# A hardware-queue fp32 front, a reordered first batch and later transposes in a beacon-attention and GEGLU kernel

## The chip, the cores and the metric

The kernel runs on one core of a Trainium2 chip. The metric is the device time of one execution in microseconds. The kernel before takes 397.61 us (median of 3 runs, 397.56 to 398.33). A run is called slow when it is over 1.5% above the fastest of the same kernel.

Five engines matter: PE (TensorE matmuls and transposes), ACT (ScalarE, here exps, gelus and copies), DVE (VectorE copies and multiplies), POOL (GpSimd: issues the casting loads and makes masks) and SP (issues plain stores and loads).

## The reference

Attention over 8 batches, 8 heads, 576 positions of 64 numbers, with 16 extra "beacon" keys that everyone sees, then a gated feed-forward block on all 4608 tokens:

```python
k_all = np.concatenate([beacon_k, k], axis=2)          # 16 + 576 keys
v_all = np.concatenate([beacon_v, v], axis=2)
scores = (q @ k_all.transpose(0, 1, 3, 2)) / np.sqrt(D)  # D = 64, causal over the 576
a = np.exp(scores - scores.max(-1, keepdims=True)); a /= a.sum(-1, keepdims=True) + 1e-09
x = (a @ v_all).transpose(0, 2, 1, 3).reshape(4608, 512)
out = (gelu(x @ w_gate) * (x @ w_val)) @ w_out           # d_ff = 1536
```

Inputs and output are fp32; the kernel multiplies in bf16.

## The kernel before

Heads are worked in pairs, four pairs to a batch, and a pair's scores come in four chunks: PE writes `s_ps` (two buffers), ACT takes the exp. Batch 0 has its q and k transposed on PE, batch 1 too (in between gate/value tiles of batch 0); later batches use DMA transposes. Each engine executes its instructions in the order in which the program gives them: this is what `keep` enforces. So an instruction that waits on PE holds everything behind it on PE.

```python
    psum_s = ctx.enter_context(tc.tile_pool(name="psum_s", bufs=2, ...))   # scores, gate/value
    psum_x = ctx.enter_context(tc.tile_pool(name="psum_x", bufs=1, ...))   # transposes, values, some outputs
    psum_o = ctx.enter_context(tc.tile_pool(name="psum_o", bufs=1, ...))   # outputs, dummies
    # ... cut ...
    def load_qk6(b, h0, h1):                     # POOL's casting loads, fp32 to bf16
        # ... cut ...
    def transpose_pe(b, m, pool, tag):           # 24 transposes of q and k, one of kb, one copy by DVE
        t_ps = pool.tile([P, 3 if tag == "x" else 2, 1024], BF16, name="t_ps", tag=tag)
        # ... cut ...
    def warm(b, m, n):                           # dummy matmuls
        w_ps = psum_o.tile([P, D_MODEL], FP32, name="w_ps", tag="o")
        for _ in range(n):
            mm(w_ps, ident, qkT[:, m, 1, 0:512], True, True)
    # ... cut ...
    load_qk6(0, 0, 2)
    by_diagonal(ident, ALU.not_equal, 1.0)
    load_kb(0)
    load_qk6(0, 2, 4)
    load_qk6(0, 4, H)
    by_diagonal(tri, ALU.is_ge, 0.0)
    load_v(0)
    for i in range(3):
        load_gate_val(i)
    load_qk6(1, 0, H)
    load_kb(1)
    load_out_w()
    load_v(1)
    transpose_pe(0, 0, psum_s, "s")
    for b in range(B):
        # ... cut: ab(m) is score chunks 0 and 1, cd(m) chunks 2 and 3, av(m) values and normalisation ...
        if b == 0:
            for m in range(NPAIR):
                ab(m)
                if m == NPAIR - 1:
                    # ... cut: masks of pairs 0 to 2 on DVE ...
                    av(0)
                    # ... cut ...
                else:
                    transpose_pe(0, m + 1, psum_x, "x")
                    # ... cut: some masks ...
                cd(m)
                if 1 <= m < NPAIR - 1:
                    warm(b, m, 5)
            # ... cut ...
            av(1, by_act=True)
            av(2, wide=True, by_act=True, direct=True)
            av(3, by_act=True, direct=True)
        # ... cut: later batches; the outputs o() of the batch before lie between their chunks ...
        for fi in range(F_TILES):                # 12 gate/value tiles of 8 matmuls
            gate_val(b, fi, kk_late=fi == 0)
            if b == 0 and 6 <= fi < 10:
                transpose_pe(1, fi - 6, psum_x, "x")
```

The softmax here doesn't subtract the row's maximum and nothing guards it: scores larger than these inputs give would overflow.

Of the kernel before, what the change touches and what calls it, by code (L numbers as in the profile page):

```python
# [7 lines left out]
P = 128  # L8
# [44 lines left out]
def kernel(  # L53
# [25 lines left out]

    ident = const.tile([P, P], BF16, name="ident", tag="ident")  # L80
    nc.vector.memset(ident, 0.0)
    ones = const.tile([P, D], BF16, name="ones", tag="ones")
    nc.vector.memset(ones, 1.0)
    wg_sb = const.tile([P, K_CHUNKS, D_FF], BF16, name="wg_sb", tag="wg_sb")
# [25 lines left out]

    qk6 = {}

    def load_qk6(b, h0, h1):
        if b not in qk6:
            qk6[b] = (
                hpool.tile([P, 2, H, 6 * D], BF16, name="qk6", tag="hT_sb"),
                npool.tile([NB, H, D], BF16, name="kb", tag="kb"),
            )
        for w, src in enumerate((q, k)):
            dma(  # L120
                qk6[b][0][0:96, w, h0:h1, :],
                src[b, h0:h1, :, :].rearrange("h (p r) d -> p h (r d)", r=6),
            )

    def load_kb(b):
        dma(qk6[b][1], beacon_k[b].rearrange("h t d -> t h d"))

    def load_keys(src, beacon, dst, b):
        dma(dst[0:NB, 0, :, :], beacon[b].rearrange("h t d -> t h d"))
# [28 lines left out]
        keep(nc.scalar.activation(out_ap, in_ap, func, **kw))  # L158


    def transpose_pe(b, m, pool, tag):
        t_ps = pool.tile([P, 3 if tag == "x" else 2, 1024], BF16, name="t_ps", tag=tag)
        qk, kb = qk6[b]

        def tr(out_ap, in_ap):
            n = in_ap.shape[0]
            keep(nc.tensor.transpose(out_ap, in_ap, ident[0:n, 0:n]))  # L167

        for w in range(2):
            for r in range(6):  # L170
                for hi in range(2):
                    tr(
                        t_ps[64 * hi : 64 * hi + 64, w, r * 96 : (r + 1) * 96],
                        qk[0:96, w, 2 * m + hi, r * D : (r + 1) * D],
                    )
        tr(t_ps[:, 1, S:SK], kb[:, 2 * m : 2 * m + 2, :])
        keep(
            nc.vector.tensor_copy(  # L178
                qkT[:, m, :, NB:SK].rearrange("p w (t r) -> p w t r", r=6),
                t_ps[:, 0:2, 0:S].rearrange("p w (r t) -> p w t r", r=6),  # L180
            )
        )
        keep(nc.vector.tensor_copy(qkT[:, m, 1, 0:NB], t_ps[:, 1, S:SK]))  # L183


    def warm(b, m, n):
        w_ps = psum_o.tile([P, D_MODEL], FP32, name="w_ps", tag="o")
        for _ in range(n):
            mm(w_ps, ident, qkT[:, m, 1, 0:512], True, True)

    def transpose_dma(b):
        q_sb, k_sb = q_ring[b % NRING], k_ring[b % NRING]
# [29 lines left out]
        if b:  # L222
            masks(b, m, c)

    def masks(b, m, c):
        expT = exp_of[b * NPAIR + m]
        for t, s_lo, _, _ in CHUNKS[c]:
            if s_lo != S_LO[t]:
                continue
            n = DIAG[t]  # L230
            d = expT[0 : KROWS[t], :, EXP_OFF[t] : EXP_OFF[t] + n]
            if b == 0:
                w = tri[0 : KROWS[t], NB : NB + n] if t == 0 else tri[0 : KROWS[t], 0:n]
                w = w.rearrange("p (o n) -> p o n", o=1).to_broadcast([KROWS[t], 2, n])
                keep(nc.vector.tensor_tensor(out=d, in0=d, in1=w, op=ALU.min))
            else:
                keep(
                    nc.gpsimd.affine_select(  # L238
                        out=d,
                        in_=d,  # L240
                        pattern=[[0, 2], [1, n]],
                        compare_op=ALU.is_ge,
                        fill=0.0,
                        base=NB if t == 0 else 0,
                        channel_multiplier=-1,
                    )
                )
# [2 lines left out]

    x_of = {}

    def attend(b, m, t, wide=False):
        i = b * NPAIR + m
        if t == AV_ORDER[0]:
            if wide:
                x_of[i] = tuple(
                    (psum_s.tile([P, 1024], FP32, name=name, tag="s"), 0, 512) for name in ("xs_ps", "zs_ps")
                )
            else:  # L260
                x_ps = psum_x.tile([P, 1536], FP32, name="x_ps", tag="x")
                x_of[i] = ((x_ps, X0, 512 - X0), (x_ps, Z0, 1024 - Z0))
        expT, v_sb = exp_of[i], v_ring[b % NRING]
        kr, first, last = KROWS[t], t == AV_ORDER[0], t == AV_ORDER[-1]
        for w, (ps, base, split) in enumerate(x_of[i]):
            for q0, q1 in ((S_LO[t], split), (max(split, S_LO[t]), S)):
                if q0 >= q1:
                    continue
                e0 = EXP_OFF[t] + q0 - S_LO[t]
                for hi in range(2):  # L270
                    mm(
                        ps[64 * hi : 64 * hi + 64, base + q0 : base + q1],
                        ones[0:kr, :] if w else v_sb[0:kr, t, 2 * m + hi, :],
                        expT[0:kr, hi, e0 : e0 + q1 - q0],
                        first and (wide or not (w == 1 and q0 == 0)),
                        last,
                        skip_group_check=True,
                    )





    def normalize(b, m, by_act=False, direct=False):
        i = b * NPAIR + m
        (x_ps, xc, _), (z_ps, zc, _) = x_of.pop(i)
        x_ps, z_ps = x_ps[:, xc : xc + S], z_ps[:, zc : zc + S]
        del exp_of[i]
        rec_sb = npool.tile([P, S], FP32, name="rec_sb", tag="rec_sb")
        x_sb = x_ps  # L290
        if not direct:
            x_sb = npool.tile([P, S], FP32, name="x_sb", tag="x_sb")
        if by_act:
            ln_sb = npool.tile([P, S], FP32, name="ln_sb", tag="zT_sb")
            act(ln_sb, z_ps, ACT.Ln)
            if not direct:
                keep(nc.vector.tensor_copy(x_sb, x_ps))
            act(rec_sb, ln_sb, ACT.Exp, scale=-1.0)
        else:
            zT_sb = npool.tile([P, S], FP32, name="zT_sb", tag="zT_sb")  # L300
            r_sb = npool.tile([P, S // 32, 1], FP32, name="r_sb", tag="r_sb")
            if not direct:
                act(x_sb, x_ps, ACT.Copy)
            keep(nc.vector.transpose(zT_sb, z_ps))  # L304
            keep(nc.vector.reciprocal(r_sb, zT_sb.rearrange("p (c o) -> p c o", o=32)[:, :, 0:1]))
            keep(
                nc.vector.transpose(  # L307
                    rec_sb.rearrange("p (c o) -> p c o", o=32), r_sb.to_broadcast([P, S // 32, 32])
                )
            )  # L310
        keep(
            nc.vector.tensor_tensor(  # L312
                out=xT_sb[:, m, b * S : (b + 1) * S], in0=x_sb, in1=rec_sb, op=ALU.mult
            )
        )


    h_of, o_of = {}, {}
# [54 lines left out]
            )  # L373
        )

    load_qk6(0, 0, 2)
    by_diagonal(ident, ALU.not_equal, 1.0)
    load_kb(0)
    load_qk6(0, 2, 4)
    load_qk6(0, 4, H)  # L380
    by_diagonal(tri, ALU.is_ge, 0.0)
    load_v(0)
    for i in range(3):
        load_gate_val(i)
    load_qk6(1, 0, H)
    load_kb(1)
    load_out_w()
    load_v(1)
    transpose_pe(0, 0, psum_s, "s")
    for b in range(B):  # L390
        u = [0]

# [10 lines left out]
            scores(b, m, 2)  # L403
            scores(b, m, 3)

        def av(m, wide=False, **kw):
            for t in AV_ORDER:
                attend(b, m, t, wide)
            normalize(b, m, **kw)

        keep(nc.scalar.preload_act_table_set(SET_EXP))
        if b == 0:
            for m in range(NPAIR):
                ab(m)
                if m == NPAIR - 1:
                    for mm_ in (0, 1, 2):
                        for c in range(4):
                            if (mm_, c) > (1, 1):
                                masks(0, mm_, c)
                    av(0)  # L420
                    for c in (0, 1):
                        masks(0, m, c)
                else:
                    transpose_pe(0, m + 1, psum_x, "x")
                    if m == 2:
                        for mm_, c in ((0, 0), (0, 1), (0, 2), (0, 3), (1, 0), (1, 1)):
                            masks(0, mm_, c)
                cd(m)
                if 1 <= m < NPAIR - 1:
                    warm(b, m, 5)  # L430
            for c in (2, 3):
                masks(0, NPAIR - 1, c)
            av(1, by_act=True)
            av(2, wide=True, by_act=True, direct=True)
            av(3, by_act=True, direct=True)
        else:
            o(6)
            ab(0)
            o(10)
# [9 lines left out]
        keep(nc.scalar.preload_act_table_set(SET_GELU))  # L449
        for fi in range(F_TILES):  # L450
            gate_val(b, fi, kk_late=fi == 0)
            if b == 0 and 6 <= fi < 10:
                transpose_pe(1, fi - 6, psum_x, "x")
            if fi == 0:
                if b + 2 < B:
                    load_qk(b + 2)
# [37 lines left out]
```

## Time and profile before

| what | before |
|---|---|
| time | 397.61 us |
| span of the profiled execution | 396.2 us |
| PE busy | 382.3 us, 97% of the span |
| first exp starts, last exp of batch 0 ends | 8.49, 24.94 us |
| dense gate/value matmuls start | 31.95 us |
| first output matmul inside batch 1, first values of batch 1 | 55.25, 62.18 us |

These are the busy times of the engines, then PE's row and the granted TensorE clock (PEclk) in 40 slices of the span, in tenths (a 9 is 90% or more), then the shares of the chain of waits that ended last. Kernel before:

```profile
PE 382.3 (97%) x3046; PEld 185.9 (47%) x3046; DVE 190.5 (48%) x304; ACT 202.2 (51%) x280; POOL 156.3 (39%) x277
...
PE   3889999999999999999999999999999999999996
...
PEclk9999999999999999999999999999999999999999
...
PE 79%; DMA 8%; POOL 3%; DVE 3%; ACT 3%; issue 2%; SPq 2%; POOLq 0%; ACTq 0%
```

Apart from the last slice, only the first three (30 us) are not full of PE work. After them the kernel is a PE stream, so a change to the first 30 us can at best start this stream earlier.

In those 30 us ACT's exps are the pace. The timeline of ACT, kernel before: start, duration, operation; in brackets how long ACT was idle before it and what it waited for (adjacent equal instructions are merged, hence x2).

```profile
8.49 1.89 ACT L158 ACTIVATE expT<-s_ps 128x1024 bf16<-128x1024 f32 x2 [6.40 <-PE s_ps L155]
10.62 1.35 ACT L158 ACTIVATE expT<-s_ps 128x928 bf16<-128x928 f32 x2 [0.24 <-PE s_ps L155]
12.26 1.89 ACT L158 ACTIVATE expT<-s_ps 128x1024 bf16<-128x1024 f32 x2 [0.29 <-PE s_ps L155]
14.55 1.35 ACT L158 ACTIVATE expT<-s_ps 128x928 bf16<-128x928 f32 x2 [0.40 <-PE s_ps L155]
17.51 3.14 ACT L158 ACTIVATE expT<-s_ps 128x1024 bf16<-128x1024 f32 x4 [1.61 <-PE s_ps L155]
21.26 1.89 ACT L158 ACTIVATE expT<-s_ps 128x1024 bf16<-128x1024 f32 x2 [0.61 <-PE s_ps L155]
```

PE's timeline of the same stretch shows the clock through durations:

```profile
7.84 1.01 PE L155 MATMUL s_ps<-qkT 64*128 64x512 bf16 x8 [1.53 <-DVE qkT L183]
...
14.61 2.32 PE L155 MATMUL w_ps<-qkT,ident 128*128 128x512 bf16 x5
16.86 1.01 PE L155 MATMUL s_ps<-qkT 64*128 64x512 bf16 x8
...
18.89 0.37 PE L155 MATMUL s_ps<-qkT 64*128 64x464 bf16 x2
...
20.83 0.60 PE L155 MATMUL s_ps<-qkT 64*128 64x512 bf16 x8
```

The same eight score matmuls take 1.01 us at 16.86 us and 0.60 us at 20.83: early on TensorE runs at half clock. The change lies before 18.89, where two 464-column matmuls take 0.37 us, as they do at full clock later; the trace's first clock record puts it at 18.6 us. The PEclk row does not show the half clock (it shows 9), because the trace has no clock record before the first change; here the durations are to be trusted. The group of five dummies at 14.61 stands in front of pair 2's score chunk at 16.86, for which ACT idles the 1.61 us. DVE's copy for that pair ended at 15.5 us, so the old kernel's own dummies may make up to about 1.4 us of its largest hole (an estimate from these times; no run takes them out).

### The profile page before, as it was taken

How to read it: one execution, taken by the hardware profiler on the slowest of the kernel's cores; microseconds unless marked ns; L12 is line 12 of the kernel's file. 1: busy time of each engine (PE TensorE's matmuls, PEld its weight loads, DVE VectorE, ACT ScalarE, POOL GpSimd, SP SyncE). 2: the span in 40 equal slices, each digit the busy share in tenths (PEclk: the TensorE clock that was granted, in tenths of full speed). 3: DMA queues.
4: the chain of work that ended last, by engine and by line, in shares of the span. 5: the costliest groups of instructions: out<-in, count | busy, mean ns of one | idle time of the engine just before them, and what ended most of it. 6: DMA issues, size and time to landing. Idle time of an engine off the chain costs nothing.

```text
span 396.2 us, 7413 instructions
## 1 busy us (share of the span) xinstructions
PE 382.3 (97%) x3046; PEld 185.9 (47%) x3046; DVE 190.5 (48%) x304; ACT 202.2 (51%) x280; POOL 156.3 (39%) x277
## 2 busy tenths in 40 slices
PE   3889999999999999999999999999999999999996
PEld 2464545544454445444544455444544455444442
DVE  1393654844375327642673338433754266332332
ACT  2775258634873379336843586347823793332210
POOL 8722395780369124931486047803400240000000
PEclk9999999999999999999999999999999999999999
DMA  7999998699129930996099915991032010000012
GB/s 91 180 206 204 175 132 97 68 169 121 55 36 156 141 79 30 120 156 84 29 107 162 89 55 57 163 137 58 28 89 59 34 45 32 0 0 29 28 53 106
DMA packets 139154, 36.24 MB, mean 91 GB/s; under 512 B 126832, under 2 KB 134512, under 8 KB 139120
## 3 DMA queue, kind: packets, MB, share of 16 engines
q0 software_dynamic: 103984, 19.14, 64.4%
q1 hardware_dynamic: 35136, 16.62, 19.3%
q8 instruction: 24, 0.39, 0.4%
q14 instruction: 10, 0.08, 0.1%
HBM read 38.27 MB, written 9.44 MB: 120 GB/s over the span
## 4 chain that ended last, share of the span: by engine, by line
PE 79%; DMA 8%; POOL 3%; DVE 3%; ACT 3%; issue 2%; SPq 2%; POOLq 0%; ACTq 0%
PE gv_ps L155 36%; PE o_ps L155 23%; PE x_ps L155 11%; PE s_ps L155 8%; DMA qkT<-k_sb_94 3%; DMA v_sb_98<-in_beacon_v_dram 2%; SPq L196 2%; ACT expT L158 2%; DMA k_sb_97<-in_k_dram 2%; POOL k_sb_97 L109 1%; PE t_ps L167 1%; DVE qkT L178 1%; POOL q_sb_96 L109 1%; PE w_ps L155 1%; DMA kb<-in_beacon_k_dram 1%
## 5 line engine op out<-in xcount | busy, mean ns | idle before, releaser
L158 ACT ACTIVATE ge_sb<-gv_ps 128x512 bf16<-128x512 f32 x108 | 64.5, 597 | 150.7 <-PE gv_ps L155 150.7
L340 DVE TENSOR_TENSOR hT_sb<-gv_ps,ge_sb 128x512 bf16<-128x512 f32 x108 | 74.7, 692 | 116.0 <-ACT ge_sb L158 116.0
L158 ACT ACTIVATE expT<-s_ps 128x1024 bf16<-128x1024 f32 (+3 forms) x128 | 103.9, 870 | 25.8 <-PE s_ps L155 25.7
L155 PE MATMUL gv_ps<-xT_sb,wg_sb 128*128 128x512 bf16 x432 | 112.2, 379 | 0.8 <-DVE xT_sb L312 0.8
L155 PE MATMUL gv_ps<-xT_sb,wv_sb 128*128 128x512 bf16 x432 | 112.2, 379 | 0.0
L238 POOL TENSOR_SCALAR_AFFINE_SELECT expT<-expT 128x256 bf16<-128x256 bf16 (+2 forms) x140 | 52.4, 388 | 142.2 <-ACT expT L158 142.1
L155 PE MATMUL o_ps<-wo_sb,hT_sb 128*128 128x512 bf16 x432 | 103.6, 380 | 0.0
L155 PEld LDWEIGHTS <-wv_sb 128*128 128x128 bf16 x432 | 42.3, 98 | 52.7 <-issue 2.7
L155 PEld LDWEIGHTS <-wg_sb 128*128 128x128 bf16 x432 | 41.9, 98 | 49.9
L155 PEld LDWEIGHTS <-hT_sb 128*128 128x128 bf16 x432 | 38.8, 98 | 46.6 <-issue 2.8
L364 DVE COPY o_sb<-o_ps 128x512 f32<-128x512 f32 x36 | 24.7, 687 | 37.9 <-PE o_ps L155 37.9
L155 PE MATMUL s_ps<-qkT 64*128 64x80 bf16 (+5 forms) x384 | 39.1, 294 | 2.7 <-DVE qkT L183 1.5
L155 PE MATMUL x_ps<-expT,ones 128*64 128x432 bf16 (+1 forms) x558 | 41.2, 243 | 0.0
L304 DVE STREAM_TRANSPOSE zT_sb<-x_ps 128x576 f32<-128x576 f32 x29 | 22.7, 781 | 29.9 <-ACT x_sb L158 29.9
L155 PEld LDWEIGHTS <-qkT 64*128 64x128 bf16 x384 | 14.8, 96 | 30.4 <-issue 21.8
L155 PEld LDWEIGHTS <-ones 128*64 128x64 bf16 (+1 forms) x578 | 23.2, 110 | 4.6
L307 DVE STREAM_TRANSPOSE rec_sb<-r_sb 128x576 f32<-128x576 f32 x29 | 22.6, 778 | 1.0
L155 PE MATMUL x_ps<-expT,v_sb_95 128*64 128x80 bf16 (+5 forms) x270 | 21.5, 245 | 1.5 <-DVE zT_sb L304 1.1
L155 PE MATMUL x_ps<-expT,v_sb_98 128*64 128x80 bf16 (+5 forms) x288 | 22.8, 246 | 0.0
L109 POOL DMA_DIRECT2D v_sb_98<-in_v_dram x20 | 17.0, 868 | 11.9 <-DMA wv_sb<-in_moe_w_val_dram 3.7
L109 POOL DMA_DIRECT2D v_sb_95<-in_v_dram x20 | 17.0, 889 | 2.5 <-DMA k_sb_94<-in_k_dram 2.3
L312 DVE TENSOR_TENSOR xT_sb<-x_sb,rec_sb 128x576 bf16<-128x576 f32 x23 | 17.4, 758 | 0.9
(51 smaller groups left out, 190.9 us busy)
## 6 DMA issues: line engine op xcount, KB each, us to landing
out_dram<-o_sb SPq DMA_DIRECT2D x36, 256.0 KB, 2.0
v_sb_95<-in_v_dram POOLq DMA_DIRECT2D x12, 128.0 KB, 7.9
wg_sb<-in_moe_w_gate_dram POOLq DMA_DIRECT2D x3, 512.0 KB, 11.6
wv_sb<-in_moe_w_val_dram POOLq DMA_DIRECT2D x3, 512.0 KB, 13.3
wo_sb<-in_moe_w_out_dram POOLq DMA_DIRECT2D x1, 1536.0 KB, 23.5
v_sb_98<-in_v_dram POOLq DMA_DIRECT2D x12, 128.0 KB, 10.6
q_sb_93<-in_q_dram POOLq DMA_DIRECT2D x12, 128.0 KB, 4.2
q_sb_96<-in_q_dram POOLq DMA_DIRECT2D x12, 128.0 KB, 4.2
```

The source lines that it names most:

```text
L109: keep(nc.gpsimd.dma_start(out=out_ap, in_=in_ap))
L155: keep(nc.tensor.matmul(out_ap, lhsT, rhs, start=start, stop=stop, **kw))
L158: keep(nc.scalar.activation(out_ap, in_ap, func, **kw))
L167: keep(nc.tensor.transpose(out_ap, in_ap, ident[0:n, 0:n]))
L178: nc.vector.tensor_copy(qkT[:, m, :, NB:SK].rearrange("p w (t r) -> p w t r", r=6), t_ps[:, 0:2, 0:S].rearrange("p w (r t) -> p w t r", r=6),)
L196: nc.sync.dma_start_transpose(out=qkT[:, :, w, c + j * P : c + j * P + n], in_=src[0:n, j, :, :].rearrange("p h d -> p (h d)"),)
L238: nc.gpsimd.affine_select(out=d, in_=d, pattern=[[0, 2], [1, n]], compare_op=ALU.is_ge, fill=0.0, base=NB if t == 0 else 0, channel_multip ...
L304: keep(nc.vector.transpose(zT_sb, z_ps))
L307: nc.vector.transpose(rec_sb.rearrange("p (c o) -> p c o", o=32), r_sb.to_broadcast([P, S // 32, 32]))
L312: nc.vector.tensor_tensor(out=xT_sb[:, m, b * S : (b + 1) * S], in0=x_sb, in1=rec_sb, op=ALU.mult)
L340: nc.vector.tensor_tensor(out=h_of[ci][:, fi, :], in0=gv_ps[:, 1, :], in1=ge_sb, op=ALU.mult)
L364: keep(nc.vector.tensor_copy(o_sb[:, ti, :], o_ps))
```

## The change

The intent: start sooner, by loading the first pair's q and k in fp32 with the two hardware queues (SP and ACT issue them) and casting on ACT and DVE; then make batch 0 one stream, in which values and normalisations of pair m lie between the score chunks of pair m+1, so that less is left after the last exp. Dummies at the start are to raise the clock early. Two of the pairs are transposed in halves, through the one buffer of `psum_o`. POOL takes over masks and therefore issues gate/value weights and batch 1's loads later. Batch 1's PE transposes move from gate/value tiles 6 to 9 to the last four tiles.

```diff
+    def transpose_half(b, m, w):
+        t_ps = psum_o.tile([P, 1024], BF16, name="t_ps", tag="o")
+        tr_part(b, m, w, t_ps)          # 12 transposes (and kb for w = 1)
+        copy_part(m, w, t_ps)           # copy by DVE
+    def warm(n, pool=None, tag="o", w=512):
+        w_ps = (pool or psum_o).tile([P, D_MODEL], FP32, name="w_ps", tag=tag)
+        for j in range(n):
+            mm(w_ps[:, 0:w], idle[:, ...], idle[:, 0:w], True, True)
 ...
-    load_qk6(0, 0, 2)
+    stage = opool.tile([P, 2, 2, 6 * D], FP32, name="stage", tag="o_sb")
+    load_kb(0)
+    for eng, w, src in ((nc.sync, 0, q), (nc.scalar, 1, k)):
+        keep(eng.dma_start(out=stage[0:96, w, :, :], in_=src[0, 0:2, :, :]...))
 ...
-    for i in range(3):
-        load_gate_val(i)
+    load_gate_val(0)
+    warm(6)
+    act(qk6[0][0][0:96, 0, 0:2, :], stage[0:96, 0, :, :], ACT.Copy)
+    keep(nc.vector.tensor_copy(qk6[0][0][0:96, 1, 0:2, :], stage[0:96, 1, :, :]))
+    transpose_first()                   # q half copied by ACT, k half by DVE
+    c(0, 0)                             # c(m, n): score chunk n of pair m
+    c(0, 1)
+    transpose_pe(0, 1)
+    mk(0, 0, 1, by_dve=True)            # masks
+    c(0, 2)
+    warm(2)
+    c(0, 3)
+    for w in range(2):
+        transpose_half(0, 2, w)
+    mk(0, 2, 3, by_dve=True)
+    c(1, 0)
+    warm(3, w=512)
+    c(1, 1)
+    warm(30, w=65)
+    c(1, 2)
+    av(0, 0, 2, 4)
+    c(1, 3)
+    mk(1, 0, 1, 2, 3)
+    load_gate_val(1)
+    av(0, 1, 3)
+    normalize_a(0, 0)
+    for w in range(2):
+        transpose_half(0, 3, w)
+    c(2, 0)
+    c(2, 1)
+    normalize_b(0, 0)
 ...  # pairs 2 and 3 in the same manner
+    mk(3, 0, 1, 2, 3)
     load_qk6(1, 0, H)
     load_kb(1)
     load_out_w()
     load_v(1)
+    normalize_by_act(0, 2)
+    av(3, *AV_ORDER)
+    normalize_by_act(0, 3, direct=True)
 ...
-            if b == 0 and 6 <= fi < 10:
-                transpose_pe(1, fi - 6, psum_x, "x")
+            if b == 0 and fi >= 8:
+                transpose_pe(1, fi - 8)
```

## The prediction

> **What bounds the kernel now.** From 32 us on it is the TensorE stream: the busy table gives PE 97% of 396.2 us, and the chain of waits is nearly all gv_ps, o_ps, s_ps and x_ps matmuls. Nothing there is changed except the place of batch 1's PE transposes. The change acts on the first 32 us. There the chain of waits runs through the first loads and kb (to 6.1 us), DVE's copy of t_ps (1.36 us), ACT's exps (16 chunks in about 13 us back to back, first at 8.49, last ending at 24.94), then a tail of values and normalisations; the last pair's xT comes at 31.9 us, where the dense gate/value matmuls start.
>
> **Front.** First q landed 3.0 us after issue (4.44). The Trainium skill ("DMA: Bandwidth & Descriptors", section on latency) gives the hardware queues a shorter first byte, 0.6 against about 1 us; this trace has only their 256 KB stores, 2.0 us to landing. I expect the fp32 stage at 3.3 to 3.9, casts of about 0.8 us (from ACT's 1.02 us for 1024 columns), first exp near 7.0: 1.5 us earlier. Six early dummy matmuls should warm PE by 5 to 9 us instead of about 19.5 (512-column score chunks: 8 matmuls in 1.01 us before that, 0.60 after), as "TensorE: Matmul & The Clock Gate" (The HAM clock gate) describes.
>
> **Middle.** I laid the traced durations out in the new order (the same layout puts the old start of gate/value at 32.0, traced 31.95). The halves of pairs 2 and 3 share one PSUM buffer, so the key half waits for DVE's query copy (0.75 us), and PE, in order, holds the next score chunk behind it: ACT should idle about 1.7 us before exp of pair 1 and 2.4 us before pair 2 (there DVE's zT, 0.78, comes first). This gives the front's gain back; the last exp ends near 26. The tail is shorter (5.5 instead of 7.0 us), since pairs 0 and 1 are already normalised. Gate/value's last xT: 31.4, i.e. 0.5 us earlier, +-1.2.
>
> **After.** Batch 1's transposes move to the last four tiles. Behind the last one, o_ps wants the same PSUM buffer and waits for DVE's copy, which in this trace ended 1.7 to 2.0 us after the transposes: +1.75 us. Batch 1's masks on POOL come only after 16 load issues behind wo's landing (47.3, masks at 59.95, values at 62.18 now). wo's landing is set by DMA volume (204 to 206 GB/s from 16 to 40 us) and hardly moves. So even if gate/value started 6 us earlier, values of batch 1 could start at best near 59: gain at most about 3 us.
>
> **Sum.** -0.5 + 1.75 = about +1.2; the layout may be pessimistic about the middle, so I put 398.3 us, range 395.4 to 400.5. Faster by over 2%: 3%; within 2%: 96%; slower: 1%.
>
> **What would show it.** First exp near 7.0. PE idle in t_ps waiting for DVE qkT at about 10 to 11 and 16 to 18 us. First full gate/value at 31 to 32. o_ps waiting 1.7 us for DVE qkT just before batch 1. POOL's first batch-1 masks still near 59 to 60. wo landing at 46 to 47. From batch 1's values on, all stages shifted by one constant.
>
> **What would make it wrong.** A gate/value start at 26 to 28 us (DVE halves off ACT's path): then POOL's masks of batch 1 bind and the time is 394.5 to 396. Late loads (gate/value weights issued behind masks on POOL leaving DMA idle): wo later, the time 400 or more. PE staying cold until 20 us: +2.

## More of the kernel before

In 32 further runs the kernel before stayed within 397.49 to 399.15 us.

Between the exps of pairs 0 and 1 ACT is idle for only 0.29 us; the largest hole is the 1.61 us before pair 2.

## The result

The changed kernel takes 408.36 us (median of 4 runs, 405.68 to 408.75): slower, by a ratio of 1.0242 (95% interval 1.0206 to 1.0279). A second set of six runs on another occasion gave 408.96 us (406.70 to 410.95) and 1.0267. A ratio here is the mean time of one kernel's fast runs over that of the kernel before's fast runs of the same rounds, so it is not quite the ratio of the medians that are quoted beside it. The prediction of 398.3 us, with a range to 400.5, was wrong by 10 us.

The page of the changed kernel, the same rows as shown of before:

```profile
PE 384.3 (95%) x3022; PEld 188.2 (46%) x3073; DVE 189.9 (47%) x296; ACT 203.2 (50%) x281; POOL 162.4 (40%) x292
...
PE   5877998999999999999999999999999999999995
...
PEclk9998998999999999999999999999999999999999
...
PE 92%; DVE 3%; ACT 2%; issue 1%; DMA 1%; DVEq 0%
```

PE's busy time is almost the same (384.3 against 382.3 us) and the span is 10.4 us longer: the loss is idle time of PE (digits 8, 7, 7 in slices 2 to 4, and the 8 of slice 7, at 61 to 71 us) and a granted clock below 0.9 in slices 4 and 7.

Where the difference arises, from the starts in the two timelines (one execution each):

| milestone | before | after | difference |
|---|---|---|---|
| first exp starts | 8.49 | 9.74 | +1.25 |
| first exp of pair 1 | 12.26 | 15.94 | +3.68 |
| first exp of pair 2 | 17.51 | 25.53 | +8.02 |
| last exp of batch 0 ends | 24.94 | 32.47 | +7.53 |
| dense gate/value starts | 31.95 | 38.91 | +6.96 |
| first output matmul in batch 1 | 55.25 | 64.04 | +8.79 |
| first values of batch 1 | 62.18 | 72.58 | +10.40 |
| end of the span | 396.2 | 406.6 | +10.4 |

The rest of the program only shifts. ACT's timeline after the change, for the same exps:

```profile
9.74 1.89 ACT L163 ACTIVATE expT<-s_ps 128x1024 bf16<-128x1024 f32 x2 [2.51 <-PE s_ps L160]
11.86 0.94 ACT L163 ACTIVATE expT<-s_ps 128x928 bf16<-128x928 f32 x1 [0.24 <-PE s_ps L160]
13.12 0.52 ACT L163 ACTIVATE expT<-s_ps 128x416 bf16<-128x416 f32 x1 [0.32 <-PE s_ps L160]
15.94 1.02 ACT L163 ACTIVATE expT<-s_ps 128x1024 bf16<-128x1024 f32 x1 [2.30 <-PE s_ps L160]
18.30 0.97 ACT L163 ACTIVATE expT<-s_ps 128x960 bf16<-128x960 f32 x1 [1.34 <-PE s_ps L160]
20.57 0.94 ACT L163 ACTIVATE expT<-s_ps 128x928 bf16<-128x928 f32 x1 [1.30 <-PE s_ps L160]
...
25.53 2.72 ACT L163 ACTIVATE expT<-s_ps 128x1024 bf16<-128x1024 f32 x3 [2.43 <-PE s_ps L160]
```

Four large holes have opened: 2.30 us before pair 1, 1.34 and 1.30 us inside it, 2.43 us before pair 2. Before the change the holes at these places were 0.29 us, none and 0.40 us, and 1.61 us. What PE did in them, from its timeline after the change:

```profile
1.34 2.74 PE L160 MATMUL w_ps<-idle 128*128 128x512 bf16 x6 [1.34 <-DVE idle L83]
5.84 0.69 PE L171 MATMUL t_ps<-ident,qk 96*64 96x96 bf16 x12 [1.76 <-ACT qk L163]
7.28 0.69 PE L171 MATMUL t_ps<-ident,qk 96*64 96x96 bf16 x12 [0.75 <-ACT qkT L163]
9.09 1.01 PE L160 MATMUL s_ps<-qkT 64*128 64x512 bf16 x8 [1.00 <-DVE qkT L190]
...
14.55 0.69 PE L171 MATMUL t_ps<-ident,qk 96*64 96x96 bf16 x12 [0.85 <-DVE qkT L188]
...
16.29 1.46 PE L160 MATMUL w_ps<-idle 128*128 128x512 bf16 x3 [0.38 <-DVE qkT L190]
17.68 0.58 PE L160 MATMUL s_ps<-qkT 64*128 64x64 bf16 x6
18.20 1.83 PE L160 MATMUL w_ps<-idle 128*128 128x65 bf16 x30
...
24.61 0.45 PE L171 MATMUL t_ps<-ident,qk 96*64 96x96 bf16 x12 [1.95 <-DVE qkT L188]
...
33.85 0.52 PE L160 MATMUL x_ps<-expT,v_sb 128*64 128x496 bf16 x4 [1.95 <-DVE x_sb L318]
...
64.04 2.06 PE L160 MATMUL o_ps<-wo_sb,hT_sb 128*128 128x512 bf16 x6 [1.77 <-DVE qkT L202]
66.03 1.01 PE L160 MATMUL s_ps<-qkT 64*128 64x512 bf16 x8
```

There are three kinds of line to read here. First, waits that block the stream: the second transpose half waits for DVE's copy of the first out of the one buffer (0.85 and 1.95 us), with the next score chunk behind it. Second, work that is in the way: the two groups of dummies at 16.29 and 18.20, 3.29 us in all, stand between the score chunks for which ACT is idle 1.34 and 1.30 us. Third, the clock: the eight matmuls of the first chunk take 1.01 us, so the six dummies have not raised it, and half clock lasts to 20.4 us; at 66.03, in the middle of the dense part, the same eight matmuls take 1.01 us again.

The windows view gives that late clock: stretch, PE and other busy times, then PEclk, the DMA share and GB/s. After the change:

```profile
32.00:36.00 4.00, 2.15 (x28) 1.60 (x29) 1.51 (x2) 1.69 (x3) 4.00 (x8) 0.76 1.17 188
36.00:40.00 4.00, 3.24 (x23) 1.66 (x21) 0.76 (x1) 3.07 (x4) 3.30 (x5) 0.82 1.28 203
...
64.00:68.00 4.00, 3.96 (x17) 1.33 (x18) 0.00 (x0) 1.32 (x2) 1.50 (x3) 0.60 1.90 121
```

Before the change all three rows show 1.00. The trace's clock records give two half-clock stretches of 3.41 us each, about 34.1 to 37.5 and 64.8 to 68.2 us, beginning 0.2 and 0.7 us after the two waits of nearly 2 us (which end at 33.85 and 64.04). They have a price: the last pair's 36 value matmuls take 2.83 us, where the same group takes 1.56 in a stretch at full clock (in the kernel lean, below).

Why these two waits and not the equally long one at 22.7 to 24.6 us? In each of the 18 traces all changes of the clock lie whole multiples of 3.41 us apart. On this grid, laid through the clock records of the changed kernel, PE's busy time is the first number after the comma:

```profile
20.41:23.82 3.41, 2.25 (x52) 1.72 (x51) 0.69 (x1) 2.11 (x3) 1.90 (x4) 1.00 0.06 9
23.82:27.23 3.41, 2.62 (x49) 1.78 (x50) 2.69 (x7) 1.70 (x2) 0.74 (x2) 1.00 0.91 135
30.65:34.06 3.41, 1.47 (x26) 0.88 (x24) 1.75 (x4) 2.97 (x5) 3.41 (x8) 1.00 0.89 119
...
61.37:64.78 3.41, 1.55 (x29) 1.04 (x30) 2.07 (x4) 1.83 (x2) 3.41 (x5) 1.00 2.15 134
```

The first wait is split between two windows, the two others fall whole into one, and only after those does the clock fall. In all 18 profiles the 16 falls after 19 us (the end of the program left out) follow windows with PE busy for 1.46 to 1.68 us; no window with 1.76 or more was followed by one, and two with 1.65 were not either.

### The profile page after: what moved, and what is told of

Read it like the earlier page. It is cut to its first block, busy times and chain, and to the rows that moved or that the text cites. A ratio compares the mean times of both kernels' runs of the same rounds, so it can differ in the third digit from the quotient of the medians.

```text
span 406.6 us, 7429 instructions
## 1 busy us (share of the span) xinstructions
PE 384.3 (95%) x3022; PEld 188.2 (46%) x3073; DVE 189.9 (47%) x296; ACT 203.2 (50%) x281; POOL 162.4 (40%) x292
## 4 chain that ended last, share of the span: by engine, by line
PE 92%; DVE 3%; ACT 2%; issue 1%; DMA 1%; DVEq 0%
PE gv_ps L160 45%; PE o_ps L160 24%; PE x_ps L160 12%; PE s_ps L160 8%; PE t_ps L171 2%; DMA stage<-in_q_dram 1%; ACT expT L163 1%; PE w_ps L160 1%; DVE qkT L188 1%; DVE qkT L197 1%; DVE hT_sb L376 0%; ACT ln_sb L163 0%; ACT ge_sb L163 0%; ACT x_sb L163 0%; ACT qk L163 0%
## 5 line engine op out<-in xcount | busy, mean ns | idle before, releaser
L267 POOL TENSOR_SCALAR_AFFINE_SELECT expT<-expT 128x256 bf16<-128x256 bf16 (+2 forms) x155 | 58.3, 387 | 160.2 <-ACT expT L163 160.1
L160 PE MATMUL gv_ps<-xT_sb,wv_sb 128*128 128x512 bf16 x417 | 110.1, 379 | 0.8
L160 PE MATMUL o_ps<-wo_sb,hT_sb 128*128 128x512 bf16 x401 | 100.8, 383 | 4.8 <-issue 2.1
L160 PE MATMUL x_ps<-expT,v_sb 128*64 128x80 bf16 (+5 forms) x576 | 46.8, 249 | 2.0 <-DVE x_sb L318 1.9
L160 PE MATMUL x_ps<-expT,ones 128*64 128x144 bf16 (+5 forms) x576 | 43.4, 247 | 0.0
L111 POOL DMA_DIRECT2D v_sb<-in_v_dram x40 | 34.0, 884 | 8.1 <-DMA qk<-in_k_dram 2.8
L160 PEld LDWEIGHTS <-v_sb 128*64 128x64 bf16 (+1 forms) x576 | 24.2, 111 | 13.1 <-issue 4.7
L160 PEld LDWEIGHTS <-qkT 64*128 64x128 bf16 x384 | 14.5, 95 | 29.5 <-issue 23.0
L111 POOL DMA_DIRECT2D q_sb<-in_q_dram x30 | 25.3, 860 | 5.9 <-DMA wo_sb<-in_moe_w_out_dram 5.6
L111 POOL DMA_DIRECT2D k_sb<-in_k_dram x30 | 25.4, 902 | 0.0
```

Source lines behind the costliest of these rows:

```text
L111: keep(nc.gpsimd.dma_start(out=out_ap, in_=in_ap))
L160: keep(nc.tensor.matmul(out_ap, lhsT, rhs, start=start, stop=stop, **kw))
L267: nc.gpsimd.affine_select(out=d, in_=d, pattern=[[0, 2], [1, n]], compare_op=ALU.is_ge, fill=0.0, base=NB if t == 0 else 0, channel_multip ...
```

## The experiments

All kernels below gave a correct result. "Starting from the changed kernel" is meant unless said otherwise. The theory at first: PE's order (waits for DVE's half copies, late transposes), a slower front and the low clock add up. The rivals: the late weight loads; or the clock alone.

### tr69: the transposes of batch 1 back in their old place

```diff
-            if b == 0 and fi >= 8:
-                transpose_pe(1, fi - 8)
+            if b == 0 and 6 <= fi < 10:
+                transpose_pe(1, fi - 6)
```

> The changed kernel, with batch 1's PE transposes put back behind gate/value tiles 6 to 9. Theory PE (in-order TensorE waits plus its clock): the 1.77 us wait of o_ps for DVE's copy of t_ps before batch 1 is gone, and with it probably the half-clock stretch of 3.4 us that followed it (64.8 to 68.2 us, about 1.8 us lost): 3.4 us faster than the changed kernel's 408.4, i.e. 404 to 406; 1.7 us faster if the half clock comes all the same. Theory LOADS (late loads from the POOL queue cost the time): batch 1's q and k then arrive too late for tile 6, PE waits for them in t_ps, and nothing is gained.

Measured: 404.77 us (403.23 to 406.49), ratio 1.0167 (1.0133 to 1.0201). The 1.77 us wait of o_ps is gone from the profile, and so is half clock near 65 us (in this execution it fell at 24.9 to 28.3 and 35.1 to 38.5 us instead of at 34). The gain in ratio, 0.0075 of 398 us against the first set of the changed kernel, is 3.0 us (4.0 against the second set): the wait, and about as much again for the clock behind it. This term of the prediction (+1.75) was right as far as it went.

### loads_up: gate/value weights issued before the masks

```diff
-    load_gate_val(0)
+    for i in range(3):
+        load_gate_val(i)
     warm(6)
 ...
-    load_gate_val(1)
-    load_gate_val(2)
```

> The changed kernel, with all three slices of gate and value weights issued in front of batch 0's masks on POOL, as before the change. Theory LOADS: DMA no longer stands idle at 20 to 24 us (18 GB/s in the changed kernel), wo lands near 47 instead of 52.3, and the kernel is about 5 us faster. Theory PE: no wait of PE in the changed kernel was for a load after the first pair, so wo lands near 47 but the time stays within 1 us of 408.4.

Measured: 407.13 us (407.11 to 410.21), ratio 1.0244 (1.0206 to 1.0282): nothing gained. The DMA engines' idle stretch (18 GB/s at 20 to 24 us in the changed kernel) became 206 GB/s, but a new one opened at 32 to 36 us (24 GB/s), and w_out landed at 50.7 us, not at the 47 expected: the hole moved behind the masks of the next loads. Between landing at 52.3 and 50.7 the time does not change, and in the changed kernel POOL's masks of batch 1 waited for ACT and not for loads. So late loads are real, and the 5 us that the theory of late loads asked for are not there; a landing at 47 was not reached in this run.

### front_sw: the old front in the new stream

```diff
-    stage = ...; two hardware-queue loads; cast by ACT and DVE; transpose_first()
+    load_qk6(0, 0, 2)
+    load_kb(0)
+    transpose_pe(0, 0)
```

> The changed kernel, with the first head pair loaded as before the change (cast by the software queue, both halves copied by one DVE instruction), the stream of batch 0 kept. If the fp32 load on hardware queues is itself a loss (stage landed 4.1 us after issue against 3.0 for the cast load, then a cast of 0.84 us and a wait of PE for ACT's copy): first exp near 8.6 to 8.9 instead of 9.74, time 0.5 to 1.5 us lower. If the front is worth its intent (rival): first exp later than 9.74 and time 1 us or more higher.

Measured: 407.10 us (403.92 to 408.93), ratio 1.0198 (1.0151 to 1.0244). The first exp came at 8.81 us, as expected, but in the profiled execution half clock struck at 24.3 to 27.7, 34.5 to 37.9 and 65.2 to 68.6 us and the last exp ended at 33.34, later than in the changed kernel. In time the result cannot be told from the changed kernel's: inconclusive. It showed that a single execution of this stream says little about one microsecond, because where half clock falls differs from execution to execution.

### b_front_hw: the new front alone, in the kernel before

Starting from the kernel before:

```diff
-    load_qk6(0, 0, 2)
+    stage = ...; two hardware-queue loads        # as in the change
 ...
-    transpose_pe(0, 0, psum_s, "s")
+    cast q by ACT and k by DVE; transpose and copy by halves (ACT, DVE)
```

> The kernel before with the new front alone: first head pair in fp32 on the hardware queues, cast by ACT and DVE, copied in halves; no early dummies, no stream. If the front is a loss by itself (in the changed kernel its first exp came 0.93 us later than with the old front): first exp at 9.3 to 9.8 instead of 8.49, time 0.8 to 1.5 us above the kernel before. Rival (the front gains, and only the stream loses): first exp before 8.4, time 0.5 us or more below.

Measured: 399.79 us (399.18 to 399.98), ratio 1.0034 (1.0019 to 1.0049). In this kernel executions agree well, and the front is a loss by itself: 1.4 us by the ratio, and the first exp is 1.39 us later than before's 8.49:

```profile
5.08 0.84 ACT L162 ACTIVATE qk<-stage 96x768 bf16<-96x768 f32 x1 [2.54 <-DMA stage<-in_q_dram]
6.71 0.65 ACT L162 ACTIVATE qkT<-t_ps 128x576 bf16<-128x576 bf16 x1 [0.79 <-PE t_ps L407]
9.88 1.89 ACT L162 ACTIVATE expT<-s_ps 128x1024 bf16<-128x1024 f32 x2 [2.51 <-PE s_ps L159]
```

The data landed at about 5.1 us, where the prediction had put the stage at 3.3 to 3.9; the cast of 0.84 is as predicted; then come two copies one behind the other.

### warm_late: dummies in the two late waits

```diff
+    warm(8)
     av(3, *AV_ORDER)
 ...
                 transpose_pe(1, fi - 8)
+                if fi == F_TILES - 1:
+                    warm(8)
```

> The changed kernel, with 8 dummy matmuls put into each of the two late PE waits (before the last pair's values, 31.9 to 33.9 us, and before batch 1's first o_ps, 62.3 to 64.0). Theory PE with clock: neither half-clock stretch (34.1 to 37.5 and 64.8 to 68.2 us) appears; values of the last pair take 1.6 instead of 2.8 us, batch 1's first part loses 1.8 us less: 2.5 to 3.3 us faster, 405 to 406. Rival (the clock follows something else, or the waits alone cost): same time or up to 0.5 us slower.

Measured: 405.81 us (405.17 to 407.20), ratio 1.0197 (1.0172 to 1.0221). The waits are still there, but filled with dummies, and in the profiled execution half clock has gone from them. Windows view of this kernel:

```profile
32.00:36.00 4.00, 3.89 (x48) 2.14 (x46) 1.51 (x2) 2.13 (x4) 4.00 (x7) 1.00 1.23 204
...
64.00:68.00 4.00, 4.00 (x28) 1.59 (x23) 0.69 (x1) 3.02 (x4) 2.06 (x6) 1.00 1.95 176
```

The gain by ratio is 0.0045 to 0.0070 of 398 us (against the two sets of the changed kernel), 1.8 to 2.8 us, and 2.6 us by the medians. So the two half-clock stretches are worth about two microseconds, and short waits caused them: to fill the same waits with useless work removes them.

### warm_front: more dummies at the start

```diff
-    warm(6)
+    warm(10)
 ...
             copy_part(0, w, t_ps[:, w, :], by_act=w == 0)
+            warm(1 + w)
```

> The changed kernel, with 10 instead of 6 dummy matmuls at the start and 1 and 2 more in the waits behind the first pair's transposes. If the cold TensorE of the first 20 us is what my layout missed: the eight matmuls of the first score chunks take about 0.6 instead of 1.01 us, first exp near 9.2, last exp near 29 instead of 32.5, time 2 to 3.5 us below 408.4. Rival (the middle is bound by the waits for DVE's copies whatever the clock): last exp after 31, time within 1 us.

Measured: 405.68 us (402.71 to 409.09), ratio 1.0223 (1.0177 to 1.0268). The run of 409.09 counts as slow and is left out of what follows. The fast runs are 402.71, 405.62 and 405.74; their mean over that of the kernel before's seven runs gives 1.0167, so the ratio is not that of these three, and the mean gain stays uncertain. The spread is the finding. The profiled execution was the fastest one, 402.71 us, and had full clock from about 6 us on (the first chunk in 0.60 us); its last exp ended at 28.72 us instead of 32.47, and its fillers between the chunks took 0.82 and 1.08 us instead of 1.46 and 1.83. The two other fast executions took 3 us more, at a mean granted clock of 0.987 against 1.000. So with this order an execution at full clock was about 3 us faster than two in which it fell at some time, and ten dummies do not secure it in every execution. They do start it: in all five profiled kernels with ten dummies at the start the clock was full by 4.4 to 6.1 us, with six in one of ten (tr69).

### before_warm and before_warm10: an early clock for the kernel before

The rival "the clock alone" says that the kernel before must gain by it too. Starting from the kernel before, with 7 and 3, or with 10 and 5 dummies:

```diff
+    warm_idle(10)
     transpose_pe(0, 0, psum_s, "s")
+    warm_idle(5)
```

> The kernel before, with 7 dummy matmuls on zeros at its start and 3 behind the first transposes, nothing else. If a cold TensorE until 19.4 us costs the kernel before as well: first score chunks in 0.6 us, gate/value start 1 to 2 us earlier, 396 to 397; no more, as the masks of batch 1 on POOL come only at about 60. Rival (the dummies only delay): 398 to 399.

> The kernel before, with 10 dummies at the start and 5 behind the first transposes. The first run with dummies (7 and 3) left TensorE cold until 17.5 us. If 4.4 us of dummies without a break are what brings the clock up (as in best1, full speed at 6.2 us): score chunks in 0.6 us from the first one, gate/value start near 30, time 396 to 397. If it is the kind of work that follows which counts: cold again soon, and 398 to 399.5.

Measured: before_warm 399.03 us (397.75 to 399.39), ratio 1.0021 (1.0002 to 1.0040), half clock until about 17.6 us; the dummies did not do it. before_warm10: 398.66 us (397.94 to 399.80), ratio 1.0011 (0.9988 to 1.0033). There the clock was full at 8.19 us, but it fell back:

```profile
1.34 3.81 PE L157 MATMUL w_ps<-idle 128*128 128x512 bf16 x10 [1.34 <-DVE idle L83]
...
8.19 0.60 PE L157 MATMUL s_ps<-qkT 64*128 64x512 bf16 x8 [0.34 <-DVE qkT L185]
...
11.66 1.01 PE L157 MATMUL s_ps<-qkT 64*128 64x512 bf16 x8 [0.84 <-DVE qkT L185]
```

Two things follow. In this execution the kernel's own work (transposes and 64-row score matmuls with short waits) did not hold the full clock: it was full from 4.4 to 11.2 us and half until 18.0. And the kernel before gained nothing from the early clock that it got. No run shows it with full clock all the way to 20 us, so the rival is weakened, not excluded. The old order runs in 397.6 us with half clock until 18.6 us; in the new one, which puts values, halves and fillers onto PE between the chunks, ACT waits for all of them.

### apart: a score chunk between the two halves

```diff
-    for w in range(2):
-        transpose_half(0, 2, w)
-    mk(0, 2, 3, by_dve=True)
+    transpose_half(0, 2, 0)
     c(1, 0)
-    warm(3, w=512)
+    transpose_half(0, 2, 1)
+    mk(0, 2, 3, by_dve=True)
     c(1, 1)
+    warm(3, w=512)
 ...  # the same for pair 3, around c(2, 0) and c(2, 1)
```

> The changed kernel, with the two half transposes of pairs 2 and 3 no longer next to each other: the next pair's score chunk stands between them, so PE has it issued while DVE copies the query half. If PE, in order, holding the score chunks behind the key half is what idles ACT (2.30 us before the exp of pair 1, 2.43 before that of pair 2): last exp 2.5 to 3.5 us earlier, near 29.5, time 2 to 3.5 us below 408.4. Rival (ACT would wait elsewhere: psum_o, values): last exp within 1 us of 32.5, same time.

Measured: 404.57 us (402.44 to 408.15), ratio 1.0175 (1.0120 to 1.0230). The last exp ended at 30.7 us (expected 29.5), and half clock came at 33.4 to 36.8 us. By the medians 3.8 us gained; by the ratios 2.7 to 3.7. ACT's 2.30 us before pair 1 became 0.18 us, though 3.16 us opened behind the fillers, which now stand together. So the waits for DVE's half copies were on the path, as the theory says; the size is known only roughly, since the spread of this kernel is 5.7 us.

### best1 and lean: the mends together, with and without the fillers

best1 is tr69, apart and warm_front together, with 8 dummies before the last pair's values and with gate/value weights and batch 1's q and k issued before the masks. lean is best1 without the two filler groups:

```diff
-    warm(3, w=512)
-    warm(30, w=65)
```

> The changed kernel with all the repairs together: batch 1's transposes behind tiles 6 to 9, halves apart, more dummies at the front and in front of the last pair's values, the gate, value and batch 1 q and k loads in front of the masks. If the pieces add (1.8 to 3.4 + 2.5 to 3.5 + 2 to 3 + 1.3): 398 to 401, gate/value start near 33. If another wait takes their place: above 402.

> The repaired kernel (best1) without the dummies in the middle (3 of 512 and 30 of 65 columns). With TensorE at full clock from 6 us they are not needed and hold the third score chunk of pair 1 back: ACT idled 1.89 us in front of that exp. Without them: last exp 1 to 1.9 us earlier than 27.8, time 398 to 399 against 399.9. Rival (they keep the clock up): half-clock stretches return, time above 400.5.

Measured: best1 399.94 us (399.32 to 400.77), ratio 1.0051 (1.0034 to 1.0068). lean 397.67 us (396.51 to 399.62), ratio 0.9984 (0.9945 to 1.0024): equal to the kernel before. The 10 us are found again, and the fillers alone account for about 2.7 of them (0.0067 of 398 us): in best1 ACT was idle 1.89 us behind them, in lean that idle time is gone and the last exp ended at 24.82 instead of 27.82 us. The fillers had their use too: the mean granted clock was 1.000 in all four executions of best1, and in lean 0.998, 0.998, 1.000 and, in the slowest (399.62 us), 0.987.

lean's first values of batch 1 start at 60.32 us, 1.86 us before the kernel before's 62.18, and yet it gains nothing. PE's list of waits between 138 and 186 us tells where that went:

```profile
PE s_ps L160 <- DMA qkT<-q_sb: 1.6, 2, 1.1
```

In the kernel before PE waits for no transfer in the same stretch. The chain behind it, from the chain of waits of lean: POOL's issues of q, k and v loads behind its masks up to 123.59 us, 8.86 us until v has landed, 7.58 us of DMA transposes, then PE at 140.07. This chain did not move forward with PE, so the earlier start is given back there. Part of my prediction's argument, that POOL's masks and loads limit what an earlier start can be worth, holds, only some batches later than I had placed it.

### best2: lean with the old front and pair 3's halves around values

```diff
-    stage = ...                         # the new front
+    load_qk6(0, 0, 2) ...               # the old one
 ...
+    transpose_half(0, 3, 0)
     av(0, 1, 3)
+    transpose_half(0, 3, 1)
     normalize_a(0, 0)
-    transpose_half(0, 3, 0)
     c(2, 0)
     c(2, 1)
-    transpose_half(0, 3, 1)
```

> Lean, with the old front for the first pair and the halves of pair 3 placed around the second part of pair 0's values, in front of its normalisation. If the list of losses is complete: first exp near 8.6, last exp near 25, gate/value start near 31, and values of batch 1 then bound by POOL's masks (about 59): 396 to 397.5, faster than both. If not: above 398.

Measured: 400.63 us (400.03 to 402.56), ratio 1.0066 (1.0037 to 1.0094): a miss. The first exp came early (8.45 us), but then PE waited 1.9 us for v to land and 1.1 us for POOL's masks, and later 1.6 us for DMA transposes. The front's microsecond did not carry through, because v and the masks were not earlier. Three of its four executions also had a granted clock of 0.987 to 0.991.

### no_fill, no_fill_tr69, no_fill_late and after_again: the fillers, and whether the parts add

What stayed open was how much the fillers cost in the changed kernel itself, at its own clock. So only they were taken out of it, alone, with tr69, and with the late dummies, beside the changed kernel as control, all on one chip:

```diff
     c(1, 0)
-    warm(3, w=512)
     c(1, 1)
-    warm(30, w=65)
     c(1, 2)
```

> The changed kernel without the two dummy groups between pair 1's score chunks (3 of 512 columns, 30 of 65 columns; in the changed kernel's trace they take 1.46 and 1.83 us of PE between 16.29 and 19.96, and ACT idles 1.34 and 1.30 us before the exps of the two chunks behind them). Theory (the fillers themselves delay the stream while the clock is low): these two ACT waits fall under 0.4 us each, the last exp ends 2 to 2.6 us earlier than 32.47 (about 30), and the time falls by about 2.5 us, to 405.5 to 406.5. Rival (fillers only fill waits that are there anyway, and keep the clock up): nothing moves or the clock drops more often, time 408 to 410.

> The same and batch 1's transposes back at tiles 6 to 9. If both costs are on the path and add: 2.5 and 3.3 us off, 402 to 403. If the earlier start is eaten by POOL's masks of batch 1: no more than either alone, 404.5 to 405.5.

> No fillers between the chunks, but 8 dummies in each of the two late waits (before the last pair's values and before batch 1's outputs): 2.5 us from the fillers and 2.6 us from the two half-clock stretches, so 403 to 404 and a profile without half clock from 30 us on. If the late half-clock stretches come whatever is done, 405.5 to 406.5.

> The changed kernel as it is, on the same chip, as the control for these three: 407 to 409.

| kernel | median, range (us) | ratio to before, 95% interval |
|---|---|---|
| after_again | 408.96 (406.70 to 410.95) | 1.0267 (1.0235 to 1.0299) |
| no_fill | 405.74 (405.56 to 408.05) | 1.0209 (1.0185 to 1.0233) |
| no_fill_tr69 | 404.23 (403.99 to 405.33) | 1.0153 (1.0136 to 1.0170) |
| no_fill_late | 405.56 (405.00 to 406.31) | 1.0183 (1.0166 to 1.0200) |

The fillers cost 2.3 us (0.0058 of 398.3 us), as expected. ACT's timeline of no_fill shows the first three exps of pair 1 back to back where 1.34 and 1.30 us of idle time were (1.04 us have opened before the fourth), and the exp of pair 2 at 23.92 instead of 25.53 us:

```profile
16.02 2.72 ACT L163 ACTIVATE expT<-s_ps 128x1024 bf16<-128x1024 f32 x3 [2.30 <-PE s_ps L160]
19.78 0.52 ACT L163 ACTIVATE expT<-s_ps 128x416 bf16<-128x416 f32 x1 [1.04 <-PE s_ps L160]
...
23.92 1.89 ACT L163 ACTIVATE expT<-s_ps 128x1024 bf16<-128x1024 f32 x2 [2.43 <-PE s_ps L160]
```

The last exp ends at 31.95 us, though, not at the 30 expected: half clock fell on 24 to 27 us in this execution. The 2.30 and 2.43 us before pairs 1 and 2 have stayed, as they must: they belong to the half copies. With the transposes moved back, 4.5 us are gained (0.0114), where 5.8 had been expected; the last output wait (1.77 us) and its clock risk are removed, and the parts add in direction, not in full. With the late dummies 3.3 us are gained (0.0084), where about 5.1 had been expected: in its profile there was no half clock past 28 us, as hoped, but there was at 24 to 27. The fillers' absence is no sufficient reason for it: tr69 and front_sw have the fillers and had it too. What these profiles share is that the wait of about 2 us before pair 2 left PE busy for only 1.5 us of one window, where in the changed kernel's first profile it was split between two. after_again shows both late stretches again, at about 33 to 36 and 63.5 to 67 us.

## Why the prediction was wrong

Two steps failed first: the front (first exp at 9.74 us, not near 7.0) and the early warm-up (half clock until 20.4 us, not until 5 to 9). The layout of the middle, which rested on both, also had no term for the fillers. In the order of the prediction's own steps:

- **What bounds the kernel** was right: a PE stream from 32 us on, so that only the start of this stream counts; and "all stages shifted by one constant" from batch 1's values on is what happened (+10.4 at 72 us, +10.4 at the end).
- **Front, "first exp near 7.0: 1.5 us earlier"**: wrong in sign. It came at 9.74, 1.25 us later. The prediction expects "the fp32 stage at 3.3 to 3.9" (read as a time from the start of the span, since 3.0 us after issue was already the software load's figure); it landed at 4.92 (q) and 5.2 us (k). It took 4.1 (q) and 4.4 us (k) from its issue, where the software load before had taken 3.0 us for q. The issue was 0.58 us earlier (0.81 against 1.39), so landing at 4.92 is 0.5 us behind 4.44. The cast of 0.84 us was predicted right. Not foreseen: the key half's transposes waited 0.75 us for ACT's copy, and at half clock. b_front_hw shows this front alone costing 1.4 us.
- **"Six early dummy matmuls should warm PE by 5 to 9 us"**: this is the step that failed and on which most of the others rested. They ended at 4.1 us, PE then idled 1.76 us, and half clock lasted until 20.4 us. The Trainium skill ("TensorE: Matmul & The Clock Gate", Part 1: The HAM clock gate) says that the array starts throttled to half rate and is released by a busy window of about 3.4 us which runs freely; six dummies of 2.74 us fill at most 80% of such a window (2.74 of 3.41 us), and the idle time behind them falls into the next; I could have seen that. The trace agrees with the window's length (stretches of 3.41 us). Counted back on this grid from the first clock record, the dummies put 2.00 us into one window and 0.74 into the next in the changed kernel's profile, and the clock stayed at half. In tr69's profile the same six dummies fell whole into one window, and did raise the clock, from about 4.4 to 7.8 us, though the first chunk took 1.01 us again. So with six dummies an early clock is luck; ten dummies of 4.4 us raised it in warm_front's profiled execution. The prediction's own list of risks gave "PE staying cold until 20 us: +2". The risk was named; the one execution with full clock throughout (402.71 against 405.62 and 405.74 us) suggests 3 us or more.
- **Middle, "last exp ends near 26"**: it ended at 32.47. The two holes it named, 1.7 and 2.4 us, measured 2.30 and 2.43: the mechanism (one PSUM buffer for the halves, the next score chunk held behind it) was right. Of the 6.5 us that it missed, 2.7 are the front (9.74 for 7.0), 2.6 are ACT's two waits behind the fillers (1.34 and 1.30), for which the text had no term at all, 0.6 is the first hole. About 0.5 us is left unassigned. no_fill shows the fillers as 2.3 us of time. The half clock runs through these terms: at full clock, in warm_front's profile, the same two waits were 0.71 and 0.35 us. Laid out again by hand afterwards, with the stage landing at 4.9 and half clock to 20 us, the same layout gives a last exp at 31.5 and gate/value at 37.2 us, an estimate from the traced durations that stands in no run; it still leaves 1.0 and 1.7 us.
- **Gate/value at 31.4**: 38.91. The tail after the last exp was to be 5.5 us and was 6.4 (38.91 less 32.47), half clock at 34 to 37.5 us being in it: the 36 last value matmuls took 2.83 instead of 1.56 us. This is a second step that I had not had in view, and warm_late shows that it and the next stretch are worth about two microseconds.
- **After, +1.75 for the late transposes**: right, 1.77 in the trace. Behind it came half clock from 64.8 us, which cost about as much again (the difference grows from 8.79 to 10.40 us up to the first values). tr69 gains 3.0 us. That the clock would fall behind this wait was not in the prediction.
- **Late loads**: the DMA gap came (18 GB/s at 20 to 24 us, w_out at 52.3 us, where 46 to 47 had been predicted) without a cost that the runs show; loads_up moved the gap without a change of time.

So the 10.4 us of the profiled execution are 1.25 of front, 6.3 between the first exp's start and the last exp's end, less 0.6 of a shorter tail, then 1.8 and 1.6 us around the late transposes. What is shown by runs: the front (1.4), the half copies (apart, about 3), the fillers (2.3 to 2.7), the late transposes with their clock (3.0), the late half clock as a whole (about 2, partly the same microseconds as tr69's). Except for the front, each of these is a difference of two ratios whose intervals together allow about 1.6 to 2.6 us either way (an estimate), so the sizes are rough and only their signs are clear. lean, in which all but the front are mended and the front runs at full clock (first exp at 8.98), is back at 397.67 us, level with before. How much of the middle an early full clock alone would give is not settled as a mean: only one fast execution shows it, since no kernel with the halves next to each other held the clock in every execution.

## What to carry to other kernels

When score chunks are what another engine waits for, everything put onto PE between them is on the critical path at the clock of that moment: here the first 18 to 21 us mostly ran at half clock, so cost it at that, dummies included. A single PSUM buffer for two transposes in a row puts the copy's latency into PE's queue; put an independent piece of work between the two. And a PE wait of 2 us in a dense stretch may cost twice: itself, and a window of half clock behind it. Here it did when the wait fell whole into one 3.41 us window (PE busy for 1.68 us of it or less), which differs from execution to execution; so take several executions before a difference of a microsecond or two is believed.

## What the Trainium skill lacked or had wrong

- "TensorE: Matmul & The Clock Gate", "Why this matters for your kernels", advises against idle gaps of PE over about 3 us. Here waits of 1.95 and 1.77 us were each followed by a half-clock stretch of 3.41 us in the profile, and in the control run again; filled with dummies, neither came (warm_late, clock 1.00). It depends on the execution: no_fill had the 1.8 us wait without the second stretch (PE busy 1.76 us of that window). What the page lacks is how busy a window must be: here the falls after 19 us follow windows with PE busy for 1.46 to 1.68 of 3.41 us. Nor does it say whether 64-row matmuls count in full; of transposes its Part 4 says that they don't count as PE-busy in the same way. In the kernel before PE was busy for all 4.00 us from 12 to 16, with transposes, 64-row score matmuls and dummies, and the clock stayed at half until 18.6; in before_warm10 it fell back at 11.2 us behind such work. That fits, but no run here separates these kinds of work.
- The same page, "Back-to-back issue gap", gives about 131 ns for a sustained 512-column matmul. Here 96 of them in the dense part took 20.84 us, 217 ns each, which is its formula for an isolated one.
- "DMA: Bandwidth & Descriptors", "Issuing engine by pattern", calls the hardware queues generally faster, and its section on latency gives 0.6 against about 1 us to the first byte. For this load, 288 KB of fp32 on each of two hardware queues at once, landing came 4.1 and 4.4 us after issue, against 3.0 us for the software load of the same q with a cast on the way. No page has this comparison for a landing.
- No page says that the profile's clock column reads 1.00 before the trace's first clock record; in both traces it did so for some 20 us in which matmul durations show half clock (1.01 against 0.60 us for eight score matmuls).
